# Four dV tiles stored by 15 of 16 DMA engines in place of three

## The chip, the cores and the metric

The kernel runs on one core of a Trainium2 chip. The metric is the device time of one execution in microseconds (us); the median of several executions is compared. Every execution moves the same bytes, 82.03 MB read from HBM and 82.03 MB written.

## The reference

The reference is one forward and backward pass of a gated mix of two branches, for a single token (batch 1, one query) with D = 640. Branch A is attention of 32 heads with a cache of 4096 keys and values per head (head size 128); branch B is a small dense layer with F = 1728 and the Mish activation.

```python
g = sigmoid((x * gate_w).sum(-1))
q = (x @ wq) per head; p = softmax(q K^T / sqrt(128)); o = p V
a = o @ wo
b = mish(B_x @ w1 + b1) @ w2
out = g * a + (1 - g) * b
# returned: out, and the gradients of x, k_cache, v_cache, wq, wo, w1, b1, w2, gate_w
```

With one query, each gradient of the cache is an outer product: dV[h] = p x dO[h] and dK[h] = ds x q[h], each 4096 x 128 in bf16, that is 1 MB per head. Reading K and V and writing dK and dV, 4 MB per head and 128 MB in all, is most of the traffic; the weights and their gradients are the rest.

## The kernel before

One head's K or V is a tile of 128 partitions x 32 x 128: partition p holds keys 32p to 32p+31, so one partition's row is 8 KB and contiguous in HBM. The heads are worked off one after another by `period(h)`. In it TensorE transposes V of head h and K of head h+1 (L587), ScalarE copies the transposes out of PSUM (L589), TensorE forms scores and products (L596, L667, L720), ScalarE takes the exponential, and VectorE writes dV of head h and dK of head h-1 as outer products in two halves each (`outer`, L612). Small jobs (projections of the next group of four heads, the gradient of wo per group, the whole of branch B) are put into free places by `slot`, which takes from a list of steps written out by hand.

Transfers have two issuers. SP issues all loads in order: per head K and V of three heads ahead (`load_k`, `load_v`, four buffers each), per group wo (`load_wo`, three buffers) and per two groups wq. POOL (GpSimd) issues the stores: dV at the end of `dv_half` (L642), dK of the head before at the end of `dk_half` (L629), the gradient of wo per group (L375, from the buffer wo_g that was loaded with wo), those of w2 and b1. A load into a buffer waits until the store out of it has landed; since SP works in order, what stands behind that load waits with it. dV and dK tiles share one pool of five buffers (tag `dVK`). The stores of the last two heads and of a few gradients at the end (dw1, most of dwq, dwq_l at L793, wo_g of the last group) go over SP.

A transfer of 128 partitions is split over 16 DMA engines, eight rows of 8 KB each. Three dV tiles, of heads 8, 17 and 26, are stored otherwise: `spread(i, dst, t)` cuts the 128 rows into two or three ranges, stored one by one, so that one range of 120, 105 or 120 rows is left for 15 engines, and the few other rows make up the rest. For i = 0 an instruction that resets the cursor of POOL's queue (L648) comes first. The other transfers on POOL's queue have 128, 64 or 16 rows.

POOL's order around the tiles, by the program: the dV tile of head 5 is followed by the store of wo_g of the first group (L375) and dK of head 5; that of head 12 by dK of head 12; that of head 17 by a store of wo_g; that of head 19 by dK of head 19 and two stores of branch B (L506, L508); that of head 26 by dK of head 26.

Of the kernel before, what the change touches and what calls it, by code (L numbers as in the profile page):

```python
# [16 lines left out]
def kernel(  # L17
# [26 lines left out]
    _, H, Sk, Dh = A_k_cache.shape  # L44
# [23 lines left out]
    dVv = out_3.rearrange("b h (p j) d -> (b h) p j d", p=P)  # L68
# [46 lines left out]
    def ring(h):  # L115
        return nc.sync if h >= H - 2 else nc.gpsimd
# [492 lines left out]
    def outer(dst, col, row, half):  # L609
        n = J // 2  # L610
        a, b = half * n, (half + 1) * n
        nc.vector.tensor_tensor(  # L612
            dst[:, a:b, :].rearrange("p j (a b) -> p j a b", b=2),
            col[:, a:b, :].unsqueeze(2).to_broadcast([P, n, Dh // 2, 2]),
            row.rearrange("p (a b) -> p a b", b=2).unsqueeze(1).to_broadcast([P, n, Dh // 2, 2]),
            ALU.mult)
# [16 lines left out]
    def dv_half(h, half):  # L633
        st = sts[h]
        if half == 0:
            st["dV"] = outs.tile([P, J, Dh], BF16, name="dV_sb", tag="dVK")
        outer(st["dV"], st["p"], gps[h // G]["qd"][:, 1, (h % G) * Dh:(h % G + 1) * Dh], half)
        if half == 1:
            if h in (8, 17, 26):
                spread(h // 9, dVv[h], st["dV"])  # L640
            else:
                ring(h).dma_start(dVv[h], st["dV"][:])  # L642

    def spread(i, dst, t):
        src = t[:].rearrange("p j d -> p (j d)")
        out = dst.rearrange("p j d -> p (j d)")
        if i == 0:
            nc.gpsimd.inc_swdge_sem([], [], mode="reset_dge_cursor")  # L648
        for a, b in (((120, 125), (0, 120), (125, 128)), ((0, 14), (14, 119), (119, 128)), ((0, 8), (8, 128)))[i]:
            nc.gpsimd.dma_start(out[a:b, :], src[a:b, :], max_dma_last_dim=J * Dh)  # L650

    def period(h):
# [12 lines left out]
        def o_part(a, b):  # L665
            for j in range(a, b):
# [31 lines left out]
        nc.vector.scalar_tensor_tensor(pj[:], in0=DP[:, 0:J], scalar=1.0, in1=e[:], op0=ALU.mult, op1=ALU.mult,  # L698
                                       accum_out=part[:])
        dv_half(h, 0)  # L700
        nc.tensor.transpose(PT, part[:].to_broadcast([P, P]), ident_f[:])  # L701
        if nxt:
# [6 lines left out]
        nc.vector.scalar_tensor_tensor(ds[:], in0=DP[:, 0:J].unsqueeze(2).to_broadcast([P, J, 2]), scalar=dd[:], in1=p_bf[:],  # L709
                                       op0=ALU.subtract, op1=ALU.mult)  # L710
        dv_half(h, 1)
        nc.vector.tensor_scalar(o_all[:, h:h + 1], O[:, 0:1], rz[:], None, ALU.mult)
        if nxt:
# [148 lines left out]
```

## Time and profile before

| | |
|---|---|
| median of 5 executions | 404.21 us (403.91 to 404.54) |
| the profiled execution, its own time | 404.1 us |
| its span, first to last instruction | 402.2 us |
| granted TensorE clock, mean | 0.921 |
| busy: PE, PEld, DVE, ACT, POOL | 295.2, 266.9, 303.3, 177.4, 45.8 us |
| DMA packets, bytes, mean rate | 28136, 164.93 MB, 410 GB/s |
| dV store, 1024 KB, issue to landing (median of 27 on POOL) | 11.4 us |
| dV store, pieces of the spread tiles | 6.5 to 15.9 us |

The span is the time from the first to the last instruction; the execution's own time has 1.9 us more around it. Busy times are of each engine's own instructions. PEld is TensorE's weight load, which overlaps its matmuls. DMA queue q1 carries SP's transfers, q0 POOL's, q8 the instruction fetches. "Landing" is the time at which the last of a transfer's 16 signals has come.

### The profile page before, as it was taken

The numbers are of one execution on the slowest core, as the hardware profiler recorded it, in microseconds if no ns is written. First come the engines' busy times: TensorE is split into PE (matmuls) and PEld (weight loads), VectorE is DVE, ScalarE is ACT, GpSimd is POOL, SyncE is SP. The second block draws the span as 40 slices with busy tenths as digits, with TensorE's granted clock in tenths as the row PEclk, the third lists the DMA queues.
The fourth block names the chain that finished last, engine by engine and source line by source line (L and its number), as shares of the span: only waits on it lengthen the run. The fifth ranks groups of instructions, "written<-read, shape, count | busy, mean of one in ns | idle before, by whom it ended". The sixth has DMA issues, their size and how long they took to land.

```text
span 402.2 us, 13607 instructions
## 1 busy us (share of the span) xinstructions
PE 295.2 (73%) x5872; PEld 266.9 (66%) x5872; DVE 303.3 (75%) x791; ACT 177.4 (44%) x411; POOL 45.8 (11%) x92
## 2 busy tenths in 40 slices
PE   0688898778888788568886988819888788888200
PEld 0588787677777777458866878718776777778200
DVE  3338766655899999657689699845999997899850
ACT  1355555334545455325543555605555455545000
POOL 0001111011121111011112112100110111111000
PEclk9999999979999999869998799957999999999655
DMA  8999999999999999999999999999999999999984
GB/s 291 419 418 401 420 423 419 418 424 425 419 423 421 422 423 416 424 426 420 424 422 421 423 425 419 417 428 422 420 420 422 414 416 420 424 419 418 425 366 188
DMA packets 28136, 164.93 MB, mean 410 GB/s; under 512 B 3164, under 2 KB 3868, under 8 KB 12204
## 3 DMA queue, kind: packets, MB, share of 16 engines
q1 hardware_dynamic: 17136, 93.41, 56.3%
q0 software_dynamic: 10880, 70.64, 42.2%
q8 instruction: 46, 0.75, 0.7%
q14 instruction: 14, 0.11, 0.1%
q10 hardware_dynamic: 60, 0.01, 0.0%
HBM read 82.03 MB, written 82.03 MB: 408 GB/s over the span
## 4 chain that ended last, share of the span: by engine, by line
DVE 35%; DMA 33%; PE 20%; ACT 5%; issue 3%; ACTq 0%; SPq 0%
DMA Kn<-in_A_k_cache_dram 32%; DVE dK_sb L612 8%; PE tr L587 8%; DVE dV_sb L612 8%; DVE junk L385 5%; ACT tT L589 4%; PE sA L667 3%; PE sB L720 3%; PE sA L596 3%; DVE junk L288 3%; DMA vec_rows<-in_gate_w_dram 1%; DVE wo_g L374 1%; DVE junk L494 1%; DVE junk L537 1%; DVE dj L707 1%
## 5 line engine op out<-in xcount | busy, mean ns | idle before, releaser
L589 ACT COPY tT<-tr 128x512 f32<-128x512 f32 x256 | 142.5, 589 | 134.9 <-PE tr L587 134.1
L596 PEld LDWEIGHTS <-tT 128*128 128x128 bf16 x2048 | 79.2, 98 | 40.4 <-ACT tT L589 34.8
L587 PE MATMUL tr<-ident_f,Kn 128*128 128x128 f32 x512 | 81.8, 298 | 12.6 <-DMA Kn<-in_A_k_cache_dram 12.6
L612 DVE TENSOR_TENSOR dV_sb<-p_bf,qd 128x2048 bf16<-128x2048 bf16 x64 | 78.0, 1219 | 0.3 <-issue 0.3
L612 DVE TENSOR_TENSOR dK_sb<-ds_bf,qd 128x2048 bf16<-128x2048 bf16 x64 | 77.8, 1217 | 0.0
L587 PE MATMUL tr<-ident_f,Vn 128*128 128x128 f32 x512 | 72.5, 277 | 0.0
L587 PEld LDWEIGHTS tr<-ident_f,Kn 128*128 128x128 f32 x512 | 61.1, 152 | 14.0 <-issue 12.8
L596 PE MATMUL sA<-qd,tT 128*128 128x48 bf16 x1024 | 48.3, 186 | 24.0 <-ACT dq_all L725 12.8
L587 PEld LDWEIGHTS tr<-ident_f,Vn 128*128 128x128 f32 x512 | 56.0, 141 | 0.0
L596 PE MATMUL sB<-qd,tT 128*128 128x48 bf16 x1024 | 46.0, 183 | 0.0
L667 PEld LDWEIGHTS <-Vn 128*128 128x128 bf16 x1024 | 30.2, 96 | 10.3 <-issue 10.3
L667 PE MATMUL sA<-e_bf,Vn 128*128 128x48 bf16 x1024 | 30.7, 183 | 7.5 <-DVE zs L687 6.0
L671 DVE TENSOR_REDUCE m<-sA 128x1 f32<-128x32 f32 x32 | 6.1, 190 | 37.3 <-PE sA L596 30.5
L629 POOL DMA_DIRECT2D out_dram<-dK_sb x30 | 17.3, 575 | 141.7 <-DVE rz L689 87.6
L720 PE MATMUL sB<-ds_bf,Kn 128*128 128x48 bf16 x1024 | 31.7, 185 | 1.4 <-DVE ds_bf L709 1.4
L642 POOL DMA_DIRECT2D out_dram<-dV_sb x27 | 14.7, 543 | 142.0 <-DVE dV_sb L612 56.3
L720 PEld LDWEIGHTS <-Kn 128*128 128x128 bf16 x1024 | 29.1, 97 | 1.6 <-issue 1.6
L288 DVE SCALAR_TENSOR_TENSOR junk<-wo_g,da_bc 128x640 bf16<-128x640 bf16 x32 | 26.3, 821 | 1.7 <-ACT da_bc L229 1.1
L385 DVE SCALAR_TENSOR_TENSOR junk<-wq_g,dq_bc 128x1024 bf16<-128x1024 bf16 (+1 forms) x25 | 25.1, 1005 | 0.2
L707 DVE TENSOR_SCALAR_CACHE_REDUCE dj<-sB,rz 128x128 f32<-128x128 f32 x32 | 11.1, 346 | 10.4 <-PE sB L701 10.4
L691 ACT ACTIVATE p_bf<-e_bf,rz 128x64 bf16<-128x64 bf16 x32 | 11.2, 350 | 13.6 <-DVE rz L689 10.6
L698 DVE SCALAR_TENSOR_TENSOR pj<-sB,e_bf 128x32 f32<-128x32 f32 x32 | 6.1, 191 | 12.6 <-PE sB L596 12.4
(152 smaller groups left out, 273.3 us busy)
## 6 DMA issues: line engine op xcount, KB each, us to landing
Kn<-in_A_k_cache_dram SPq DMA_DIRECT2D x32, 1024.0 KB, 23.6
Vn<-in_A_v_cache_dram SPq DMA_DIRECT2D x32, 1024.0 KB, 28.1
out_dram<-dK_sb POOLq DMA_DIRECT2D x30, 1024.0 KB, 12.3
out_dram<-dV_sb POOLq DMA_DIRECT2D x27, 1024.0 KB, 11.4
wq_g<-in_A_wq_dram SPq DMA_DIRECT2D x4, 1280.0 KB, 22.9
wo_g<-in_A_wo_dram SPq DMA_DIRECT2D x8, 640.0 KB, 14.9
out_dram<-wo_g POOLq DMA_DIRECT2D x7, 640.0 KB, 11.7
out_dram<-dwq_t SPq DMA_DIRECT2D x4, 896.0 KB, 18.2
```

The lines of the kernel that those rows point to most:

```text
L288: nc.vector.scalar_tensor_tensor(junk[:, 0:D], in0=wos[g][:, i, :], scalar=1.0, in1=da_bc[:], op0=ALU.mult, op1=ALU.mult, accum_out=gp["do ...
L385: nc.vector.scalar_tensor_tensor(junk[:, c0:c1], in0=wqs[w][:, rc, c0:c1], scalar=1.0, in1=dq_bc[:, w * WG * Dh + c0:w * WG * Dh + c1], op ...
L587: nc.tensor.transpose(tp[:, t, :], flat[:, k * P:(k + 1) * P], ident_f[:])
L589: nc.scalar.copy(sb[:].rearrange("p a b -> p (a b)"), tp[:].rearrange("p a b -> p (a b)"))
L596: nc.tensor.matmul(out[:, 2 * k:2 * k + W], lhsT=tb[:, t, par, :], rhs=vec[:, par, :].unsqueeze(1).to_broadcast([P, W // 2, 2]), start=(pa ...
L612: nc.vector.tensor_tensor(dst[:, a:b, :].rearrange("p j (a b) -> p j a b", b=2), col[:, a:b, :].unsqueeze(2).to_broadcast([P, n, Dh // 2, 2]),
L629: ring(h).dma_start(dKv[h], st["dK"][:])
L642: ring(h).dma_start(dVv[h], st["dV"][:])
L667: nc.tensor.matmul(O, lhsT=vts[h][:, j, :], rhs=st["e"][:, j:j + 1].to_broadcast([P, W]), start=(j == 0), stop=(j == J - 1))
L691: nc.scalar.activation(p_bf[:], e[:].unsqueeze(2).to_broadcast([P, J, 2]), ACT.Copy, scale=rz[:])
L707: nc.vector.tensor_scalar(dj[:], PT, rz[:], None, ALU.mult, ALU.add, accum_out=dd[:])
L720: nc.tensor.matmul(DQ, lhsT=kts[h][:, j, :], rhs=ds[:, j, 0:1].to_broadcast([P, W]), start=(j == 0), stop=(j == J - 1))
```

## The change

The condition picks the heads 5, 12, 19 and 26 in place of 8, 17 and 26, and the ranges are chosen by `i % 3`, so that the fourth tile uses the first set of ranges again and resets the cursor first. On POOL's queue this makes 101 instructions of 98: three pieces for head 5 (with a reset), three for head 12, two for head 19, three for head 26 (with a reset); heads 8 and 17 become single stores. No other engine's instructions change in kind or order.

```diff
         if half == 1:
-            if h in (8, 17, 26):
-                spread(h // 9, dVv[h], st["dV"])
+            if h % 7 == 5 and h < H - 3:
+                spread(h // 7, dVv[h], st["dV"])
             else:
                 ring(h).dma_start(dVv[h], st["dV"][:])
 
     def spread(i, dst, t):
         src = t[:].rearrange("p j d -> p (j d)")
         out = dst.rearrange("p j d -> p (j d)")
-        if i == 0:
+        if i % 3 == 0:
             nc.gpsimd.inc_swdge_sem([], [], mode="reset_dge_cursor")
-        for a, b in (((120, 125), (0, 120), (125, 128)), ((0, 14), (14, 119), (119, 128)), ((0, 8), (8, 128)))[i]:
+        for a, b in (((120, 125), (0, 120), (125, 128)), ((0, 14), (14, 119), (119, 128)), ((0, 8), (8, 128)))[i % 3]:
             nc.gpsimd.dma_start(out[a:b, :], src[a:b, :], max_dma_last_dim=J * Dh)
```

## The prediction

> **What bounds the kernel now.** I read the page's share of each engine first, then the DMA queues, the time cut into stages, the DMA issues with their landings, and last the landing signals one by one. The page:
>
> ```profile
> PE 295.2 (73%) x5872; PEld 266.9 (66%) x5872; DVE 303.3 (75%) x791; ACT 177.4 (44%) x411; POOL 45.8 (11%) x92
> DMA  8999999999999999999999999999999999999984
> q1 hardware_dynamic: 17136, 93.41, 56.3%
> q0 software_dynamic: 10880, 70.64, 42.2%
> q8 instruction: 46, 0.75, 0.7%
> ```
>
> No compute engine is above 75%. The two data queues (q1: SP's transfers, q0: POOL's stores) and the instruction fetches together fill 99.2% of sixteen engines' time. The windows of time (columns: length, then PE, PEld, DVE, ACT, POOL busy, clock, DMA share, GB/s) say the same and show the end:
>
> ```profile
> 330.00:375.00 45.00, 38.15 (x805) 34.68 (x802) 39.76 (x94) 23.08 (x53) 6.03 (x9) 1.00 1.01 421
> 375.00:388.00 13.00, 1.86 (x34) 1.21 (x30) 11.57 (x39) 0.54 (x2) 0.00 (x0) 0.54 1.01 422
> 388.00:402.00 14.00, 0.27 (x1) 0.09 (x1) 0.40 (x2) 0.26 (x1) 0.00 (x0) 0.50 0.56 220
> ```
>
> DMA is full up to 388 us; then 14 us follow with all compute done (DVE 0.40 us) and DMA only 56% busy. Some DMA engines are finished while others still work. Which, the landing signals tell: every transfer raises its semaphore 16 times, once per engine's share, and the trace has each time. For the last half of dK of head 31 (issued at 382.06) the shares land at 388.4 to 388.8 (five engines), then spread over 389.8 to 395.6, and the last at 397.99; for the final transfer, dwq_l, the last share lands at 401.12, 2.3 us after the one before it. One engine is behind all others, and SP, which waits for whole landings, is held by it:
>
> ```profile
> SPq L375 <- DMA out_dram<-dV_sb: 8.8, 1, 8.8
> SPq L793 <- DMA out_dram<-dwq_t: 2.0, 1, 2.0
> ```
>
> To see whether it ever rests, I strung the packet records into engines: on one engine a packet starts 3 to 4 ns before its predecessor's end, which gives 16 strings. The last one is idle for 0.14 us in all between 30 and 398 us. It is slow: it moved 25.7 GB/s, the others 26.3 to 26.7, and 181 of its 8 KB packets took over 330 ns (at most 38 on any other), where the normal one takes 309. So the end of this kernel is one number: the sum of the slowest engine's work. An engine with no idle time gives back every microsecond that is taken off it, until the next engine is the last.
>
> **What the spread tiles do in the trace of before.** In the strings at head 8 that same engine carries two 8 KB rows of the tile (in 4 KB packets of 159 ns), at head 17 two, at head 26 one, in place of eight; of the others some carry nine, the rest eight. This is what consecutive placement from a reset cursor gives: 5 rows on engines 0-4, 120 on 5-15 and 0-3, 3 on 4-6; then 14 on 7-4, 105 on 5-3, 9 on 4-12; then 8 on 13-4, 120 on 5-3. Engine "4" gets 2, 2 and 1 rows: 19 fewer than 24. The landing signals confirm the place. From the last load landed ahead of a spread to the first landed behind it, the last share's lag behind the eighth goes from 4.4 to 2.3 us (head 8), 4.8 to 2.9 (head 17), 8.2 to 6.3 (head 26): 1.9 to 2.1 us per tile. Between spreads it grows again.
>
> (The Trainium skill, "DMA: Bandwidth & Descriptors", section on why a DMA increments its semaphore by 16, gives this placement for POOL's transfers, k engines from a round-robin cursor, but also reports an exception: ceil(rows/16) rows per engine from engine 0. By the exception engine 15 would get no row of a 5/120/3 tile; the strings show two rows on the skipped engine, so here the cursor holds.)
>
> **Part 1: four tiles for three.** The patterns go 0, 1, 2 and again 0 with its own reset. The added tile costs the slow engine two rows instead of eight. Taken off: 8 x 309 ns = 2.47 us (2.56 at its own mean of 320 ns). Put on: 4 x 159 = 0.64 us plus about 14 completion packets of 9 ns, 0.13, together 0.77. Net 1.70 to 1.79 us; I take 1.7. The other engines: those with nine rows 18 x 159 + 7 x 9 ns = 2.92 against 2.47, so +0.45 us; those with eight +0.13. At the end the next engine stands 2.3 us ahead of the slow one; it comes to 1.85 to 2.2 us below today's end, still under the slow one's 1.7. So the slow engine stays last, with 0.1 to 0.5 us to spare, and the end moves by the whole 1.7 us.
>
> (A rule speaks against this: the skill's same page, in its rules for kernel authors, says to use all 16 engines and not to split one transfer into partition ranges, since they share the engines. By that rule the tile costs nine rows where eight stood, and the sum would be +0.45 us, 404.6. The landing lags above, down by 1.9 to 2.1 us per tile, speak for the skip.)
>
> **Part 2: other heads.** The spreads leave heads 8 and 17 and go to 5, 12 and 19; head 26 stays. With an engine that never rests, the order of its work doesn't move its end. What the pieces are moved past is POOL's queue:
>
> ```profile
> 81.85 0.53 POOL L642 DMA_DIRECT2D out_dram<-dV_sb  x1 [5.83 <-DVE dV_sb L612]
> 87.97 0.53 POOL L375 DMA_DIRECT2D out_dram<-wo_g  x1 [5.59 <-DVE wo_g L374]
> 117.67 1.94 POOL L650 DMA_DIRECT2D out_dram<-dV_sb  x3 [3.87 <-DVE b_acc L489]
> 219.51 1.84 POOL L650 DMA_DIRECT2D out_dram<-dV_sb  x3 [4.34 <-DVE dV_sb L612]
> ```
>
> Three pieces hold POOL for 1.9 us where one store holds it 0.53; behind a spread at head 5 or 12 stands a store some 5 us later, so 1.4 us are covered by POOL's wait; if not, it would cost up to 1.4 us of one store's start. The reset instruction has no row of its own: the L650 group of three with reset took 1.94, without 1.84, so about 0.1 us, on POOL, hidden likewise. Each piece also waits for the landing of the transfer eight before it; eight transfers are about 40 us and a landing takes 10 to 16, so nothing waits. The dV buffer is freed by the last piece (13.6 us after issue against 11.4); it is wanted again two to three heads later, over 20 us, so DVE doesn't wait.
>
> SP is where order could count. At heads 5 and 17 a wo_g store follows the tile, and SP waits for its landing before it loads the next wo, with K and V loads queued behind: five waits of 7.5 to 15.7 us. At head 5 the store lands at 97.55, one share 1.3 us after the rest: with the spread ahead the slow share comes 1.7 earlier, the others 0.13 to 0.45 later, so SP goes on about 1 us sooner. At head 17 the skip is gone, and the landing at 238.47 may come up to 1.7 us later. K and V loads issued at 225 land at 243.96 and 249.19, so 5 us or more of loads lie in the queue then and cover it: cost nil. Without that cover it would cost up to 1.7 us.
>
> **Sum.** The profiled execution took 404.1 us, its span 402.2, so 1.9 lie around the span. 404.1 - 1.7 = 402.4. The median, 404.21, lies 0.11 above that execution: 402.5 for the median.
>
> **Rivals.**
> 1. *The gain is not kept (no change).* Either the second reset, at head 26 with stores in flight, leaves the cursor elsewhere, so that the last tile gives the slow engine eight or nine rows, not two; then heads 5, 12 and 19 save 19 rows as three tiles do today, and the time is 404.1 to 404.5. Or the cover at head 17 fails, which returns the 1.7: 404.2. Against: the reset at head 8 worked with stores in flight too, and the DMA share is 1.01 in every window.
> 2. *SP's loads are held (slower).* The stores issued just after the head 8 spread took 13.3 us to land, the one before it 10.1. If the wo_g store of head 5 lands 3.3 us later for the same reason, SP's wo load and the K and V loads behind it (98.33) go 3.3 us later. This decides only if less than 3.3 us of loads are then queued; the price is all of it on every engine: 404.2 - 1.7 + 3.3 = 405.8. Against: K and V loads in flight then land at 99.96, 104.84 and later, over 6 us.
> 3. *The next engine takes over (smaller gain).* The 46 instruction packets fill 0.7% of 16 x 402.2 us, 45 us, so 1.0 us each. If one more falls on the engine that is second now, it ends 0.85 to 1.2 us below today's end in place of 1.85 to 2.2: 403.0 to 403.4.
>
> **How the numbers follow.** About 0.2%, 0.8 us, can be told from no change. Forecast, 0.70: 402.0 to 403.0 (1.7 with 0.5 for the spread of the five runs, 403.91 to 404.54, and for the per-tile lags of up to 2.1). Rival 3, 0.10, still faster. Rival 1, 0.13, the same. Rival 2, 0.07, slower. Faster 0.80, same 0.13, slower 0.07. The range from 401.9 to 404.1 takes in the forecast, rival 3 and the lower part of rival 1.
>
> **What would show it.** Right: the last shares at the end lie within about 0.5 us of the next ones where 2.3 stood; the skipped engine carries 7 rows of four tiles; DMA share stays full to 388. Wrong: a window with a DMA share clearly under 1 ahead of 385 us (loads held), or a last share that still lags by over 2 us (the skip missed).

## The result and the profile after

The changed kernel takes 402.69 us (median of 26 executions, 402.06 to 405.5) where the kernel before takes 404.25 (51 executions, 403.67 to 404.69): 1.56 us less. The ratio of the means is 0.9968, 95% interval 0.9962 to 0.9974, which is 1.29 us, since a few executions of the changed kernel run to 405.5. The prediction was 402.5 us, within 401.9 to 404.1.

One thing has to be known before the profile is read: the execution that was profiled took 404.07 us (span 402.3), 1.4 above its kernel's median. I therefore had the same kernel profiled a second time (run "again"): that execution took 402.70 us, its span 400.9. First the page of the first profile:

```profile
PE 299.6 (74%) x5872; PEld 271.5 (67%) x5872; DVE 303.8 (76%) x791; ACT 177.6 (44%) x411; POOL 47.2 (12%) x94
DMA  7999999999999999999999999999999999999985
q1 hardware_dynamic: 17136, 93.41, 56.2%
q0 software_dynamic: 11104, 70.64, 42.3%
q8 instruction: 46, 0.75, 0.7%
```

POOL has two instructions more and 1.4 us more of busy time, q0 moves the same bytes in 224 packets more, the compute engines do what they did. The windows of time of the same profile:

```profile
330.00:375.00 45.00, 36.99 (x787) 33.31 (x784) 39.77 (x94) 22.37 (x52) 6.01 (x9) 0.99 1.01 421
375.00:388.00 13.00, 1.61 (x26) 0.99 (x25) 10.31 (x37) 0.26 (x1) 0.00 (x0) 0.50 1.01 421
388.00:402.00 14.00, 0.00 (x0) 0.00 (x0) 0.00 (x0) 0.00 (x0) 0.00 (x0) 0.50 0.60 239
```

The DMA engines are full to 388 us, as before, so no load was held. The last 14 us are fuller (0.60 where 0.56 stood). SP's waits at the end are those of before:

```profile
SPq L375 <- DMA out_dram<-dV_sb: 8.8, 1, 8.8
...
SPq L793 <- DMA out_dram<-dwq_t: 1.8, 1, 1.8
```

POOL's timeline (start, duration, then in brackets the wait ahead of it) shows what the three pieces cost, and that the store behind them still waits for VectorE:

```profile
81.96 1.92 POOL L650 DMA_DIRECT2D out_dram<-dV_sb  x3 [5.59 <-DVE dV_sb L612]
88.22 0.58 POOL L375 DMA_DIRECT2D out_dram<-wo_g  x1 [4.35 <-DVE wo_g L374]
...
163.56 1.84 POOL L650 DMA_DIRECT2D out_dram<-dV_sb  x3 [3.87 <-DVE dV_sb L612]
...
326.75 1.92 POOL L650 DMA_DIRECT2D out_dram<-dV_sb  x3 [3.88 <-DVE m L315]
```

Following the packets as the prediction did, the slow engine carries two rows of the tile of head 5, two of head 12, one of head 19 and two of head 26: seven.

Now the second profile, its digits and its end (the last line ends where its span ends):

```profile
DMA  7999999999999999999999999999999999999995
```

```profile
375.00:388.00 13.00, 1.61 (x26) 0.99 (x25) 8.49 (x36) 0.25 (x1) 0.00 (x0) 0.50 1.01 423
388.00:400.90 12.90, 0.00 (x0) 0.00 (x0) 0.00 (x0) 0.00 (x0) 0.00 (x0) 0.50 0.63 251
```

The remaining bytes go into 12.9 us at a share of 0.63 instead of 14 us at 0.56. The landing signals name the reason. "Next" is the distance of the last share but one:

```
                    last half of dK, head 31      dwq_l
                    last share   next             last share   next
before              397.99       -2.4             401.12       -2.3
after, 404.07 us    397.96       -1.1             401.20       -1.2
after, 402.70 us    396.68       -0.6             399.82       -0.5
```

In the usual execution (402.70) no share is left 2.3 us behind. Which engine ends last comes from the strings, followed back from their end. In the 402.70 us execution it is still the slow engine, only 0.5 us behind the next: that next engine stands 0.45 us later than before (399.29 against 398.84), the slow one 1.30 us earlier (399.82 against 401.12). In the 404.07 us execution the slow engine ends 1.2 us ahead of the end (400.02 against 401.20), and an ordinary engine ends last. There many engines had slow packets between 240 and 280 us: over all 16, packets took 15.5 us more than packets of their size otherwise take, against about 1 us in a usual 10 us, and 4.8 us of that fell on the engine that ends last. Where such packets come from the trace does not show. The 402.70 us execution has 10.2 us of them in the same 40 us, at most 2.5 us on one ordinary engine, which still ends 0.7 us ahead. The trace of before has a stretch too (280 to 330 us, 14.1 us). There the ordinary engines had 2.3 us to spare; now they have 0.5 us or less. That this is why executions now spread more (402.06 to 405.5 against 403.67 to 404.69) is a reading that one slow execution supports; it is not shown.

### The profile page after: what moved, and what is told of

Read it like the earlier page. It is cut to its first block, busy times and chain, and to the rows that moved or that the text cites. A ratio compares the mean times of both kernels' runs of the same rounds, so it can differ in the third digit from the quotient of the medians.

```text
span 402.3 us, 13611 instructions
## 1 busy us (share of the span) xinstructions
PE 299.6 (74%) x5872; PEld 271.5 (67%) x5872; DVE 303.8 (76%) x791; ACT 177.6 (44%) x411; POOL 47.2 (12%) x94
## 4 chain that ended last, share of the span: by engine, by line
DVE 35%; DMA 28%; PE 24%; ACT 6%; issue 3%; ACTq 0%; DVEq 0%
DMA Kn<-in_A_k_cache_dram 26%; PE tr L587 10%; DVE dK_sb L612 9%; DVE dV_sb L612 8%; ACT tT L589 5%; DVE junk L385 4%; PE sA L667 4%; PE sA L596 3%; PE sB L720 3%; DVE junk L288 2%; DVE junk L537 2%; DVE junk L494 1%; DMA vec_rows<-in_gate_w_dram 1%; DVE dj L707 1%; PE sB L596 1%
## 5 line engine op out<-in xcount | busy, mean ns | idle before, releaser
L596 PEld LDWEIGHTS <-tT 128*128 128x128 bf16 x2048 | 80.4, 98 | 40.2 <-ACT tT L589 34.7
L587 PE MATMUL tr<-ident_f,Vn 128*128 128x128 f32 x512 | 74.7, 282 | 0.0
L596 PE MATMUL sA<-qd,tT 128*128 128x48 bf16 x1024 | 49.4, 188 | 23.6 <-ACT dq_all L725 12.6
L587 PEld LDWEIGHTS tr<-ident_f,Vn 128*128 128x128 f32 x512 | 57.9, 145 | 0.0
L720 PE MATMUL sB<-ds_bf,Kn 128*128 128x48 bf16 x1024 | 32.7, 187 | 1.4 <-DVE ds_bf L709 1.4
L720 PEld LDWEIGHTS <-Kn 128*128 128x128 bf16 x1024 | 30.0, 98 | 1.6 <-issue 1.6
L642 POOL DMA_DIRECT2D out_dram<-dV_sb x26 | 14.1, 544 | 135.8 <-DVE o_all L712 50.1
L691 ACT ACTIVATE p_bf<-e_bf,rz 128x64 bf16<-128x64 bf16 x32 | 11.2, 350 | 13.0 <-DVE rz L689 10.2
```

The lines of the kernel that those rows point to most:

```text
L587: nc.tensor.transpose(tp[:, t, :], flat[:, k * P:(k + 1) * P], ident_f[:])
L596: nc.tensor.matmul(out[:, 2 * k:2 * k + W], lhsT=tb[:, t, par, :], rhs=vec[:, par, :].unsqueeze(1).to_broadcast([P, W // 2, 2]), start=(pa ...
L691: nc.scalar.activation(p_bf[:], e[:].unsqueeze(2).to_broadcast([P, J, 2]), ACT.Copy, scale=rz[:])
L720: nc.tensor.matmul(DQ, lhsT=kts[h][:, j, :], rhs=ds[:, j, 0:1].to_broadcast([P, W]), start=(j == 0), stop=(j == J - 1))
```

## The experiments

Theory A, the prediction's: the slow engine always has work, so each spread tile takes a fixed time off the end until another engine is last. The rivals are named in the expectations. Every kernel below is the changed one with the edit shown. Times are medians, with the range and the ratio to the kernel before (404.15 to 404.26 in the three groups of runs).

**No spread tile** (none).

```diff
-            if h % 7 == 5 and h < H - 3:
+            if False:
```

> No spread tile at all: every dV tile is stored in one piece. Theory A (one slow DMA engine that never rests sets the end): against the kernel before, the slow engine gets back 19 rows in three tiles, about 1.75 us per tile, so 404.25 + 5.2 = 409.5 (409.0 to 410.2); its last share lags the next one at the end by 7 us or more. Rival B (the spread only rearranges equal work, the end has another cause): 404.25 within 0.5.

Measured: 410.06 us (409.94 to 410.59, 4 runs), ratio 1.0147 (1.0133 to 1.0161). Its page:

```profile
DMA  8999999999999999999999999999999999999953
...
q0 software_dynamic: 10288, 70.64, 41.6%
```

The last two slices (10.2 us each) are at 5 and 3 tenths: more and more engines have finished while one goes on. At the last half of dK the last share lands 8.6 us after the next, where 2.4 stood with three tiles. So the three tiles of before are worth 410.06 - 404.22 = 5.84 us, 1.95 each. That is the figure for a tile while the slow engine is far behind, and it is more than the 1.7 of the prediction.

**The rows taken from another engine** (other). Four tiles, each with its reset; the ranges put the gap two engines further on.

```diff
-        if i % 3 == 0:
+        if True:
...
-        for a, b in (((120, 125), (0, 120), (125, 128)), ((0, 14), (14, 119), (119, 128)), ((0, 8), (8, 128)))[i % 3]:
+        for a, b in ((125, 128), (0, 120), (120, 125)):
```

> Four spread tiles at the heads of the change, each with a reset and with the ranges 3, 120 and 5 rows, so that the engine two places ahead of the slow one is skipped and the slow one gets nine rows each time. Theory A: 36 rows on the slow engine instead of 7 in the changed kernel and 32 with no spread: no spread (409.5) + 4 x 0.45 = 411.3 (410.6 to 412). Rival (fewer engines per store as such is what helps): 402.7.

Measured: 411.68 us (411.19 to 411.84, 4 runs), ratio 1.0182 (1.0168 to 1.0196), and the last share of dK's last half 9.5 us behind the next. Relieving an engine that is not the slow one is worse than no spread at all, by 1.62 us or 0.40 per tile: the slow engine now carries nine rows, and the prediction had +0.45 for nine. It is the particular engine that counts, not the number of engines or of pieces.

**No second reset** (oneset).

```diff
-        if i % 3 == 0:
+        if i == 0:
```

> The changed kernel without the second reset of the cursor, so the ranges of the tile of head 26 start where the third tile left the cursor, at the skipped engine itself, and skip the engine four places further on. Theory A: the slow engine gets nine rows of that tile, 25 - 7 = 18 rows saved in all against 19 in the kernel before: 404.25 + 0.3 to 0.5, so 404.5 to 404.8. Rival (any engine may be skipped, or the reset does nothing): 402.7 as the changed kernel.

Measured: 405.07 us (404.56 to 405.59, 9 runs), ratio 1.0021 (1.0011 to 1.003). POOL's timeline and the windows:

```profile
326.62 1.86 POOL L650 DMA_DIRECT2D out_dram<-dV_sb  x3 [3.88 <-DVE m L315]
```

```profile
375.00:388.00 13.00, 1.62 (x26) 0.99 (x25) 10.17 (x37) 0.25 (x1) 0.00 (x0) 0.50 0.98 411
388.00:402.00 14.00, 0.00 (x0) 0.00 (x0) 0.00 (x0) 0.00 (x0) 0.00 (x0) 0.50 0.56 223
```

The three pieces without a reset hold POOL for 1.86 us, with it 1.92: the reset costs 0.06 us. Without it the whole gain is gone and a little more (+0.85 us against before): the slow engine carries nine rows of the tile of head 26, and the last share of dwq_l lands at 401.94, 2.7 us behind the next. The median is 0.27 us above Theory A's range (404.5 to 404.8); this excess is not accounted for. This kernel is what the prediction's first rival would have looked like. So the reset places the fourth tile's rows.

**Heads 5, 12 and 19 only** (three): the moved heads without the added tile.

```diff
-            if h % 7 == 5 and h < H - 3:
+            if h in (5, 12, 19):
```

> Only three spread tiles, at heads 5, 12 and 19, each in the place that the change gives it; head 26 in one piece. Part 2 of the change without part 1. Theory A: three tiles of ranges 0, 1, 2 take off the same 19 rows as before, 404.2 (403.8 to 404.7). Rival D: the tile at head 26 is missed, 405 to 406.

Measured: 404.37 us (404.07 to 404.53, 11 runs), ratio 1.0002 (0.9993 to 1.001), next share -2.4 at the end as before. Moving tiles costs nothing that can be measured, SP's waits at heads 5 and 17 included. The fourth tile is the whole change: 404.37 - 402.79 = 1.58 us.

**Five tiles, and six** (five, six; six at heads 1, 6, 11, 16, 21, 26).

```diff
-            if h % 7 == 5 and h < H - 3:
-                spread(h // 7, dVv[h], st["dV"])
+            if h in (3, 9, 15, 20, 26):
+                spread((3, 9, 15, 20, 26).index(h), dVv[h], st["dV"])
```

> Five spread tiles (heads 3, 9, 15, 20, 26; ranges 0, 1, 2, 0, 1). Theory A: with four tiles the slow engine is about level with the next, so a fifth tile takes 1.75 us off an engine that is no longer last and puts 0.13 to 0.45 on the others: 402.5 to 403.1, as with four or a little more. Rival C (the slow engine is still last by far with four): 400.9 to 401.3.

> Six spread tiles (heads 1, 6, 11, 16, 21, 26; ranges 0, 1, 2, 0, 1, 2). With no tile 410.06, with three 404.22, with four 402.69, with five 402.04, the gain per tile falls from 1.95 to 0.65 us. Theory A (the slow engine is no longer last, the others get 0.13 to 0.45 us per tile): the sixth tile gains nothing, 402.0 to 402.6. Rival C (the slow engine is still the last one in most executions): 401.4 or less.

Measured: five 402.04 us (401.85 to 402.47, 5 runs), ratio 0.9946 (0.9933 to 0.996); six 402.12 (402.0 to 402.26, 5 runs), ratio 0.9946 (0.9934 to 0.9958). The page and the windows of five:

```profile
DMA  7999999999999999999999999999999999999996
```

```profile
375.00:388.00 13.00, 1.42 (x22) 0.89 (x22) 8.11 (x34) 0.25 (x1) 0.00 (x0) 0.50 0.99 414
388.00:402.00 14.00, 0.00 (x0) 0.00 (x0) 0.00 (x0) 0.00 (x0) 0.00 (x0) 0.50 0.56 222
```

The last slice is at 6 tenths where none's is at 3. The next share stands 0.4 us before the end with five tiles, 0.0 with six. So tiles one to three are worth 1.95 us each, the fourth 1.6, the fifth 0.65 to 0.75, the sixth nothing. Theory A's range for five (402.5 to 403.1) was missed, and so was rival C's (400.9 to 401.3): with four tiles the slow engine is still last by 0.5 us in the execution of 402.70 us, and that is about what the fifth tile takes. In the strings the slow engine ends 1.2 us ahead of the end with five tiles and 3.3 us ahead with six, with an ordinary engine last, so the sixth has nothing left to win. Five is the version that beats both kernels.

**The same kernel again** (again): what it showed is told above; 402.79 us (402.24 to 402.98, 5 runs), ratio 0.9961 (0.9948 to 0.9974).

> The changed kernel once more, beside the next three and for a second profile: 402.7 (402.1 to 403.3). Theory A: the skipped engine is no longer the last by 2.3 us at the end; which engine is last differs from execution to execution.

**Four tiles, all early** (early).

```diff
-            if h % 7 == 5 and h < H - 3:
-                spread(h // 7, dVv[h], st["dV"])
+            if h in (1, 3, 5, 7):
+                spread((1, 3, 5, 7).index(h), dVv[h], st["dV"])
```

> Four spread tiles at heads 1, 3, 5 and 7, same ranges and resets as the changed kernel. Theory A (only the sum of the slow engine's work counts, not when it is done): as the changed kernel, 402.7 (402.2 to 403.3). Rival D (the late tile counts, because it shortens the lag that SP waits for at the end): the slow engine has fallen back by the end, 404 to 406.

Measured: 404.79 us (403.48 to 406.71, 12 runs), ratio 1.0022 (1.0006 to 1.0038). Theory A is wrong here by 2.1 us: the fourth tile's gain is gone, and a little more. The profiled execution is the shortest of the twelve (403.48 us); even there the windows are those of a kernel with three tiles:

```profile
375.00:388.00 13.00, 1.61 (x26) 0.99 (x25) 9.61 (x37) 0.25 (x1) 0.00 (x0) 0.50 0.99 412
388.00:402.00 14.00, 0.00 (x0) 0.00 (x0) 0.00 (x0) 0.00 (x0) 0.00 (x0) 0.50 0.55 220
```

The last share lands 1.8 us behind the next. At 132.69 us the share that comes first of a V load is 12.6 us ahead of the last, so the relieved engine runs far ahead in SP's queue after the tiles. Yet in the strings it has no more than 0.3 us of idle time.

**Does the place count, or the distance between tiles?** Four tests: one tile early (one_early, head 3), one late (one_late, head 26), four late (late, heads 14, 18, 22, 26), five late (five_late, heads 10, 14, 18, 22, 26). The edit is that of early with these heads, for example:

```diff
-            if h in (1, 3, 5, 7):
-                spread((1, 3, 5, 7).index(h), dVv[h], st["dV"])
+            if h in (14, 18, 22, 26):
+                spread((14, 18, 22, 26).index(h), dVv[h], st["dV"])
```

> One spread tile only, at head 3. With no spread tile the time was 410.06 us, with three 404.22, so 1.95 us per tile, and with one tile the slow engine is still last by some 2.5 us, so that nothing else can hide what it saves. Theory A (place does not count): 408.1 us (407.7 to 408.5). Rival D (a tile that is spread early loses part of its saving on the way): 408.6 to 410.1, nearer to 409 if half is lost as with the four early tiles (404.8 where 402.7 was due).

> One spread tile only, at head 26. Theory A: 408.1 us (407.7 to 408.5), the same as the one at head 3. Rival D: 408.1 or less, and at least 0.5 us under the one at head 3.

> Four spread tiles at heads 14, 18, 22 and 26 instead of 5, 12, 19 and 26. Theory A (the slow engine is always busy, so only the sum of its work counts): the place costs nothing, 402.7 us (402.3 to 403.2). Rival D (the rows must be taken from the slow engine where the end is near, because something in the middle of the kernel ties the engines together again; the four tiles at heads 1, 3, 5 and 7 gave 404.8): as good as the even spacing or better, 401.5 to 402.7. Rival E (what cost the early tiles is that they stand close together, whatever the place): 404 to 405, since here they stand four heads apart rather than seven.

> Five spread tiles at heads 10, 14, 18, 22 and 26 instead of 3, 9, 15, 20 and 26 (402.04 us). Theory A: 402.0 us (401.7 to 402.4), since the place does not count and the other engines are as far as there. Rival D (late tiles keep more of their saving): 401.0 to 401.8. Rival E (close spacing costs): 403 to 404.5.

Measured:

| kernel | median (range, runs) | ratio, 95% interval |
|---|---|---|
| one_early | 407.79 (407.52 to 408.45, 4) | 1.009 (1.0077 to 1.0103) |
| one_late | 408.39 (408.06 to 408.57, 4) | 1.0102 (1.0089 to 1.0115) |
| late | 403.71 (402.89 to 404.74, 11) | 0.9988 (0.9979 to 0.9997) |
| five_late | 402.20 (401.75 to 405.39, 12) | 0.9963 (0.9946 to 0.9979) |

One tile early saves 2.27 us (410.06 - 407.79), one late 1.67, both against a median from another group of runs (their kernels before: 404.22 and 404.15); their intervals overlap and their mean is A's 1.95. So an early tile keeps what it saves, and rival D, that only late rows count, has fallen. Late, 403.71, lies between A's range (to 403.2) and rival E's (from 404). By E, close spacing costs: four tiles two heads apart take 404.79, four heads apart 403.71, seven apart 402.7, which fits; but five tiles four heads apart take 402.20, as A had it (402.0, its range to 402.4), and E's 403 to 404.5 is missed. In the profiled execution of late the end has another shape than in early: the last three shares land within 0.8 us and the window of 375 to 388 us is full.

```profile
375.00:388.00 13.00, 1.99 (x32) 1.27 (x29) 11.56 (x39) 0.54 (x2) 0.00 (x0) 0.50 1.01 424
```

That execution had 18.2 us of slow packets between 240 and 250 us, a stretch like that in the first profile of the changed kernel. So late has a possible explanation, seen in one execution: with little held in reserve, such stretches reach the end. Early has none. What costs the four early tiles 2 us stays open.

## Why the prediction was right, and where it was not

- **The bound.** Right. One engine of sixteen sets the end: none and other move it by 5.84 us and 7.46 us with the same bytes on the same queues and the same compute. The slow engine is there in every trace I followed, on several chips: between 318 and 376 us it moves 24.9 to 25.3 GB/s, the others 26.2 to 26.6 where no stretch of slow packets lies. From 31 to 398 us, in seven later runs that were followed that far, it moves 25.3 to 25.4 GB/s, with 236 to 269 of its 8 KB packets over 330 ns and no idle time; the prediction read 25.7 and 181 in before. One small misreading there: the first five shares of the last half of dK land within 388.4 to 389.1, not 388.8. (The Trainium skill, "DMA: Bandwidth & Descriptors", section on latency and other measured facts, says that engines 7 and 15 are usually slower and guesses at POOL's descriptor rings as the cause, so for POOL's transfers alone. Here it is one engine, and its 8 KB packets take 326 ns on POOL's queue and 326 on SP's there in the first profile, so both are slowed.)
- **The placement.** Right: seven rows in four tiles, 2, 2, 1 and 2, in both profiles, and oneset shows that the second reset is needed. (This is the cursor rule of the skill's same page, cited in the prediction. For six the rows were not followed tile by tile; there the slow engine ends 3.3 us ahead of the end, where five leaves it 1.2, so the sixth tile relieved it too.)
- **The saving of a tile.** Mis-sized: 1.7 was taken, 1.95 was measured for tiles one to three. The prediction had the better number in its hands, the landing lags of 1.9 to 2.1, and used the sum of packets at 309 to 320 ns. Near the end the slow engine's 8 KB packets on POOL's queue average 326 ns in the first profile and 332 in the second; eight of these less 0.77 are 1.84 to 1.89 us. The last 0.1 is not accounted for. The fourth tile, the one predicted, moved the end by 1.56 to 1.58 us by the medians, so the predicted 1.7 is within 0.15 of it. Why the fourth gives 0.4 less than the average of the first three is not settled: the slow engine's own packets differ from execution to execution (325 to 334 ns on POOL's queue between 318 and 376 us).
- **Who is last.** Right in the one usual execution that was profiled: the slow engine was to stay last with 0.1 to 0.5 us to spare, and at 402.70 us it does, with 0.5; the next engine stands 0.45 us later, the upper end of the 0.13 to 0.45. In the execution of 404.07 us it was wrong: an ordinary engine is last and the slow one ends 1.2 us ahead. That looks like the third rival, whose cause is one added instruction fetch of 1.0 us; but that engine had 4.8 us of slow packets between 240 and 280 us, enough by themselves. The prediction had no term for such stretches.
- **Moved heads, SP and POOL.** Right: three gives 404.37 against 404.26. The pieces hold POOL 1.92 us where 1.94 was read, and the wo_g store behind them still waits 4.35 us for VectorE. The second rival (loads held, 405.8) did not happen: the DMA share is 1.01 up to 388.
- **"The order of its work doesn't move its end."** Right for the seven heads' spacing, for five tiles and for a single tile; wrong for the four tiles at heads 1 to 7 (404.79). The clause was too general, and its failure is not explained.
- **The rule against partition ranges.** The skill's advice to use all 16 engines would have given 404.6 by the prediction's working. It fails here (402.69). Other shows where it would hold: with the gap put on an ordinary engine a tile loses 0.40 us. My reading is that the advice suits engines that are alike, and one of these sixteen is not.

## What to carry to other kernels

When the DMA share is full nearly to the end and then falls while compute has finished, look at the landing of each of the 16 shares: a last share that lags by more than the others spread among themselves is one engine's backlog, and work taken off that engine comes back in full until the next engine is level. Stop there: the fifth piece of relief gave 0.65 to 0.75 us where the first three gave 1.95 each, and the sixth nothing. A kernel without reserve may also spread more from run to run: the changed kernel, late and five_late reach 404.7 to 405.5 in single executions, but five and six, with 5 runs each, stay within 0.6 and 0.3 us, so this is not settled. Place each partial transfer from a known cursor, since the same rows on a shifted cursor cost more than they save.

## What was not expected of the hardware

- Stretches of 10 to 50 us in which packets on several engines take longer, 10 to 22 us more over the 16 engines, at varying times (240 to 280 us in both profiles of the changed kernel, 240 to 250 in late, 280 to 300 in none, with 21.9 us). The trace of before has one too (14.1 us), and there the slow engine is last all the same.
- The instruction fetches (46 packets of about 1.0 us) fall on about half of the engines. Engines without them end up to 8 to 11 us ahead, so "the next engine" is one of those that fetch.
- Four tiles close together early in the kernel (heads 1, 3, 5 and 7; 404.79) give no more than three spread out (404.22 to 404.26 in the kernel before), though one early tile gives 2.27 us. Open.
